# Transposing x by DMA for duos 1 to 3, with a new order of the work, in a fused sliding-window attention and highway layer

## The chip, the core and the metric

The kernel runs on one core of a Trainium2 chip. A core has five engines that run in parallel, each with its own queue of instructions, taken strictly in order: TensorE (PE in the profile; its weight loads are PEld), VectorE (DVE), ScalarE (ACT), GpSimd (POOL) and SyncE (SP), which here only issues DMAs. GpSimd issues DMAs too, beside its arithmetic. TensorE writes into PSUM; the other data lies in SBUF. The metric is the time of one execution in microseconds on the device, the median of several runs.

## The reference

Attention over a window of 128 keys with a bias that falls linearly with distance, followed by a highway layer over the rows of its output:

```python
# q, k, v: (8, 8, 576, 64); rel = query position - key position
scores = scale * q @ k.T - slopes[h] * abs(rel)
scores = where((rel >= 0) & (rel < 128), scores, -1e9)
x = softmax(scores) @ v            # then (batch, seq, heads*dim): x is 4608 x 512
H = maximum(x @ w_h, 0)
T = 1 / (1 + exp(-(x @ w_t + b_t)))
out = T * H + (1 - T) * x
```

## The kernel before

**Tiling.** Two batch rows make a "duo"; there are four (m = 0 to 3). A duo is worked in stages: duo 0 in four small ones ("abcd"), duos 1 to 3 in two each ("A", "B"), ten in all, counted by `stage_no` from 0. A stage covers some query blocks of both rows and all eight heads, two heads at a time.

**Loads.** GpSimd issues the loads of q, k (L110), their last 64 rows (L115) and v (L122), which turn f32 into bf16 on the way. q and k have two buffers each, so duo m reuses those of duo m - 2.

**Attention.** TensorE transposes q and k (L270, L256), VectorE and ScalarE copy them out of PSUM (L282, L289, L295), TensorE forms scores (L328), ScalarE exponentiates (L344), VectorE multiplies by a mask that also holds part of the bias (L363), TensorE multiplies with v and a column of ones (L386), and VectorE divides by the sum ("norm", L402 and L403). The last norm of a stage completes its x, a tile of 128 rows by 4 or 5 blocks by 512.

**Highway layer, block by block of 128 rows.** Stage 'A' has 4 blocks, 'B' 5; duo 0 has 9 in its four stages, so there are 36. For each block:

- x is transposed, because TensorE contracts over partitions: four 128x128 transposes on TensorE into one PSUM buffer (`f_x`, L426) and one copy on ScalarE into an `xt` buffer (`f_xe`, L435).
- Z, the gate's input, is four matmuls with w_t (L460) and one that adds the bias (L462); H is four with w_h (L443). Each takes a PSUM buffer of its own.
- VectorE forms uu = max(H, 0) - x (L450), ScalarE tt = tanh(Z/2) (L468), GpSimd 0.5 tt + 0.5 (L473; for the last stage's blocks but the first on VectorE), VectorE uu * tt (L478), GpSimd uu + x into an `ot` buffer (L484; for the very last block on VectorE).
- SP stores the block with four DMAs of 64 KB (L500), or with two of 128 KB (L492) for the block that holds the last 64 rows of both batch rows.

**Buffers.** PSUM has 4 buffers for all of it; `xt` has 5, `uu`, `tt`, `ot` and x have 3 each. A new `ot` must wait until the store of the third last one has landed.

**What sets the order.** Each piece of work is entered as a node with its engine, a cost in nanoseconds, a due time, its inputs and the buffer that it takes. `plan` (L698) places the nodes: it keeps a clock per engine, and on each engine picks, among the pieces that could start within a margin `LOOKS` of the earliest, the one with the lowest due time plus its kind's `SHIFT` (L765). The instructions are then written out in that order, and each engine executes its own list in order. `DMA_X` (L52) names the stages whose x is transposed by SP's DMA instead. It is empty, so this branch of the nodes is not taken:

```python
if stage_no in DMA_X:                                   # L661
    node(("x", kb), "SP", 450 * n, t - 1.3 * dt, lambda kb=kb: f_xd(*kb), alln,
         take="xt", uses=[xo], land=1000 * n)
else:
    node(("xp", kb), "PE", 350 * n, t - 1.0 * dt, lambda kb=kb: f_x(*kb), alln, ...)
    node(("x", kb), "ACT", (590, 1020)[two], t - 0.9 * dt, lambda kb=kb: f_xe(*kb), ...)
```

`alln` is the list of all four norms of the stage, so no block of a stage is transposed before its last norm.

Of the kernel before, what the change touches and what calls it, by code (L numbers as in the profile page):

```python
# [14 lines left out]
def kernel(  # L15
# [33 lines left out]
        "d": ((3, 3, 0), (3, 4, 128), (4, 4, 192)),  # L49
    }  # L50
    ORDER = ("abcd", "AB", "AB", "AB")
    DMA_X = ()  # L52

    HOME = {"A": ("A", 0), "B": ("B", 0), "a": ("A", 0), "b": ("A", 256), "c": ("B", 0), "d": ("B", 256)}

# [17 lines left out]
    xp = ctx.enter_context(tc.tile_pool(name="x", bufs=BUFS["x"]))  # L73
# [339 lines left out]
    def f_xd(m, kind, gi):  # L413
        bs, n, x = grp(m, kind, gi)
        xt = fx.tile([P, 2, NCK, P], BF16, name="xt")
        XT[m, kind, gi] = xt
        for i in range(n):
            nc.sync.dma_start_transpose(out=xt[:, i], in_=x[:, i, :])
# [86 lines left out]
    def node(key, eng, cost, prio, emit, deps=(), take=None, uses=(), land=0, n=1):  # L505


        nodes[key] = (eng, cost, prio, emit, [d for d in deps if d in nodes],
                      take, tuple(uses), land, n)
# [37 lines left out]
    for m in range(ND):  # L547
# [56 lines left out]
        for kind in ORDER[m]:  # L604
# [3 lines left out]
            for g in range(H // 2):  # L608
# [15 lines left out]
                for hl in range(2):  # L624
                    h = 2 * g + hl
# [30 lines left out]
            for gi, bs in enumerate(GROUPS[kind]):  # L656
                t, n = ffn_pos, len(bs)
                dt = n * FFN_T
                ffn_pos += dt
                kb, xo, two = (m, kind, gi), ("nrm", (m, kind, 0)), n == 2  # L660
                if stage_no in DMA_X:  # L661
                    node(("x", kb), "SP", 450 * n, t - 1.3 * dt, lambda kb=kb: f_xd(*kb), alln,
# [35 lines left out]
    def plan(shift, look):  # L698
# [64 lines left out]
        return sorted(order, key=lambda o: o[0]), max(clock.values())  # L763

    SHIFT = {  # L765
        "exp": 88.43, "g": -18.62, "h": 0.52, "msk": 18.93, "nrm": -67.88, "o": -47.94,
        "pv": -1.59, "qk": -10.75, "s": -3.22, "st": 29.24, "t": -30.24, "te": -24.78,
        "th": 3.83, "tl": 0.89, "tr": -0.44, "u": -52.27, "v": 2.76, "x": -21.95,
        "xp": -1.21, "z": -1.38,
    }  # L770
    LOOKS = {"PE": 339, "ACT": 61, "DVE": 175, "POOL": 297, "SP": 936}
    order, end = plan(SHIFT, LOOKS)

    with tc.manual_schedule():
# [30 lines left out]
```

The softmax here doesn't subtract the row's maximum and nothing guards it: scores larger than these inputs give would overflow.

## Time and profile before

| | us |
|---|---|
| median of 3 runs | 185.63 (184.53 to 186.93) |
| the profiled execution, in all | 185.63 |
| its span, first to last instruction | 183.9 |
| TensorE busy | 155.0 (84%) |
| VectorE busy | 141.6 (77%) |
| ScalarE busy | 127.8 (69%) |
| GpSimd busy | 121.5 (66%) |
| L426, four transposes of x per block | 144 instructions, 14.1 |
| L435, their copy out of PSUM | 36, 21.0 (586 ns each) |
| stores L500 | 128 issues, 421 ns median on SP, 1.8 us to land |

The span is what the profile covers; the execution takes 1.7 us more. Busy times of TensorE overlap with its own pipeline, so the cost of a group there is better read from the distance between its neighbours than from its durations. In a row of the timeline stand the start, the length, the engine, the line, the operation with its tiles, and in brackets how long the engine had been idle before it and what ended that. SPq is SP's queue issuing DMAs. In the chain of waits each row is a start, a length, and what the time went to.

### The profile page before, as it was taken

Reading aid. Unit: us, or ns where it says so; the run is one execution under the profiler, and the core shown is the slowest. Engines: PE = TensorE matmul, PEld = TensorE weight load, DVE = VectorE, ACT = ScalarE, POOL = GpSimd, SP = SyncE. Lnnn points to the kernel's source line nnn. Section 1 sums busy time; section 2 is a strip of 40 time slices with the busy share of each in tenths; the row PEclk is TensorE's granted clock in tenths of the full one; section 3 lists DMA queues with packets and bytes.
Section 4 is the critical chain, followed back from the end, with each engine's and each line's share of the span. In section 5 each row is a group of like instructions: output and inputs, shape, how many; then the busy total and the mean of one; then the engine's idle time right before and its main releaser. Section 6 shows DMA issues by size and latency. Waiting matters only on the chain.

```text
span 183.9 us, 5244 instructions
## 1 busy us (share of the span) xinstructions
PE 155.0 (84%) x2132; PEld 93.9 (51%) x2132; DVE 141.6 (77%) x253; ACT 127.8 (69%) x178; POOL 121.5 (66%) x132
## 2 busy tenths in 40 slices
PE   0286886779999957997999999999998999999950
PEld 0264655655564524675554565665444666555510
DVE  5339885699999893697688999799899788866770
ACT  2558595753889953879779889786998888445510
POOL 7994123979999945984269953544487787667540
PEclk9999999999999996999999999999999999999995
DMA  4999999999999999999997994142212322243543
GB/s 157 225 187 198 200 199 176 138 132 92 127 207 228 210 200 205 135 187 225 208 135 96 178 159 90 45 103 61 57 45 74 93 66 74 74 103 99 137 128 94
DMA packets 70167, 25.50 MB, mean 139 GB/s; under 512 B 48128, under 2 KB 65024, under 8 KB 70144
## 3 DMA queue, kind: packets, MB, share of 16 engines
q0 software_dynamic: 62832, 14.68, 113.6%
q1 hardware_dynamic: 7312, 10.49, 21.3%
q8 instruction: 16, 0.26, 0.6%
q14 instruction: 7, 0.06, 0.1%
HBM read 30.41 MB, written 9.44 MB: 217 GB/s over the span
## 4 chain that ended last, share of the span: by engine, by line
PE 38%; DMA 26%; DVE 16%; POOL 7%; ACT 5%; issue 3%; SPq 1%; POOLq 0%; DVEq 0%; ACTq 0%
DMA kl<-in_k_dram 24%; PE ps L460 10%; PE ps L443 9%; DVE pt L363 6%; PE ps L386 6%; PE ps L270 5%; PE ps L328 5%; DVE x L403 4%; POOL ot L484 3%; DMA out_dram<-ot 3%; ACT pt L344 2%; PE ps L462 2%; DVE uu L450 2%; POOL ql L110 2%; PE ps L426 2%
## 5 line engine op out<-in xcount | busy, mean ns | idle before, releaser
L344 ACT ACTIVATE pt<-ps,bias 128x1024 bf16<-128x1024 f32 (+1 forms) x80 | 73.4, 951 | 9.1 <-PE ps L328 8.4
L484 POOL TENSOR_TENSOR ot<-uu,x 128x512 f32<-128x512 bf16 x35 | 49.7, 1421 | 30.4 <-DVE uu L478 28.9
L363 DVE TENSOR_TENSOR pt<-pt,mk 128x2048 bf16<-128x2048 bf16 (+1 forms) x40 | 47.8, 1210 | 0.7 <-ACT pt L344 0.5
L460 PE MATMUL ps<-wT,xt 128*128 128x512 bf16 x144 | 38.0, 387 | 1.2 <-DVE uu L450 0.7
L443 PE MATMUL ps<-wH,xt 128*128 128x512 bf16 x144 | 37.2, 380 | 0.6 <-DVE uu L450 0.3
L122 POOL DMA_DIRECT2D va<-in_v_dram x20 | 22.2, 1117 | 14.3 <-DMA kl<-in_k_dram 8.2
L450 DVE SCALAR_TENSOR_TENSOR uu<-ps,x 128x512 bf16<-128x512 f32 x36 | 24.8, 688 | 7.7 <-PE ps L443 7.3
L468 ACT ACTIVATE tt<-ps 128x512 f16<-128x512 f32 x36 | 21.5, 598 | 11.6 <-PE ps L462 11.1
L328 PE MATMUL ps<-qt,kt 64*128 64x256 bf16 (+2 forms) x384 | 27.2, 254 | 1.8 <-DVE kt L295 1.4
L473 POOL TENSOR_SCALAR tt<-tt 128x512 f16<-128x512 f16 x32 | 23.1, 722 | 5.6 <-ACT tt L468 5.5
L435 ACT COPY xt<-ps 128x512 bf16<-128x512 bf16 x36 | 21.0, 586 | 8.1 <-PE ps L426 7.2
L403 DVE TENSOR_TENSOR x<-ps,rd 128x256 bf16<-128x256 f32 (+3 forms) x40 | 25.5, 637 | 1.4
L386 PEld LDWEIGHTS <-pt 128*128 128x128 bf16 (+1 forms) x576 | 21.2, 101 | 8.0 <-issue 1.8
L386 PE MATMUL ps<-va,pt 128*128 128x65 bf16 (+1 forms) x576 | 24.1, 196 | 1.3 <-ACT kt L295 0.4
L295 ACT COPY kt<-ps 128x1024 bf16<-128x1024 bf16 x13 | 13.1, 1012 | 14.4 <-PE ps L270 8.4
L289 DVE COPY qt<-ps 128x1024 bf16<-128x1024 bf16 x16 | 10.9, 687 | 14.2 <-PE ps L270 10.9
L478 DVE TENSOR_TENSOR uu<-uu,tt 128x512 bf16<-128x512 bf16 x36 | 16.6, 462 | 4.9 <-POOL tt L473 2.9
L270 PE MATMUL ps<-ident,ql 128*64 128x128 bf16 (+1 forms) x320 | 13.3, 242 | 8.3 <-DMA ql<-in_q_dram 7.5
L443 PEld LDWEIGHTS <-xt 128*128 128x128 bf16 x144 | 12.1, 97 | 14.4 <-issue 2.8
L460 PEld LDWEIGHTS <-xt 128*128 128x128 bf16 x144 | 12.4, 99 | 13.7 <-issue 3.9
L328 PEld LDWEIGHTS <-kt 64*128 64x128 bf16 x384 | 12.8, 97 | 12.6 <-issue 7.0
L270 PE MATMUL ps<-ident,kl 128*64 128x128 bf16 (+1 forms) x320 | 12.8, 242 | 6.6 <-DMA kl<-in_k_dram 5.6
(46 smaller groups left out, 127.9 us busy)
## 6 DMA issues: line engine op xcount, KB each, us to landing
out_dram<-ot SPq DMA_DIRECT2D x128, 64.0 KB, 1.8
va<-in_v_dram POOLq DMA_DIRECT2D x16, 256.0 KB, 10.8
ql<-in_q_dram POOLq DMA_DIRECT2D x3, 1024.0 KB, 14.6
kl<-in_k_dram POOLq DMA_DIRECT2D x3, 1024.0 KB, 18.8
ql<-in_moe_w_h_dram SPq DMA_DIRECT2D x1, 1024.0 KB, 5.8
out_dram<-ot SPq DMA_DIRECT2D x8, 128.0 KB, 2.4
ql<-in_q_dram POOLq DMA_DIRECT2D x4, 128.0 KB, 5.8
kl<-in_k_dram POOLq DMA_DIRECT2D x4, 128.0 KB, 5.9
```

The source lines that it names most:

```text
L122: nc.gpsimd.dma_start(out=VA[m % 2][0:n, c, :, :, 0:D].rearrange("s r h d -> s (r h) d"), in_=v[2 * m : 2 * m + 2, :, c * P : c * P + n, : ...
L270: nc.tensor.transpose(out=pt[r * D : (r + 1) * D, c : c + n], in_=L[ps, r, nh * hs + hl, t * D : (t + 1) * D], identity=ident[ps, ps],)
L328: nc.tensor.matmul(out=sc[:, r, o + off : o + off + w_], lhsT=KT[i][rows, h, j * P : (j + 1) * P], rhs=rhs, start=not add, stop=not add or ...
L344: nc.scalar.activation(out=PT[m, home, h // 2][:, h % 2, :, c0 : c0 + W], in_=SC[m, kind, h][:, :, o : o + W], func=ACTF.Exp, bias=BIAS[:, ...
L363: nc.vector.tensor_tensor(out=o, in0=o, in1=mk.to_broadcast([P, 2, rep, W]), op=ALU.mult,)
L386: nc.tensor.matmul(out=av[rows, hl, n * (D + 1) : (n + 1) * (D + 1)], lhsT=pt[:, hl, r, off : off + (D if narrow else P)], rhs=va[:, j, r, ...
L403: nc.vector.tensor_tensor(out=x.rearrange("p b (h d) -> p h b d", h=2), in0=av[:, :, :, 0:D], in1=rd[:, :, 0:nb].to_broadcast([P, 2, nb, D ...
L443: nc.tensor.matmul(out=AH[m, kind, gi][:, i, :], lhsT=XT[m, kind, gi][:, i, c, :], rhs=wH[:, c, :], start=c == 0, stop=c == NCK - 1)
L450: nc.vector.scalar_tensor_tensor(out=uu[:, 0:n, :], in0=AH[m, kind, gi][:, 0:n, :], scalar=0.0, in1=x, op0=ALU.max, op1=ALU.subtract,)
L460: nc.tensor.matmul(out=az, lhsT=XT[m, kind, gi][:, i, c, :], rhs=wT[:, c, :], start=c == 0, stop=False)
L473: eng.tensor_scalar(out=tt, in0=tt, scalar1=0.5, scalar2=0.5, op0=ALU.mult, op1=ALU.add)
L484: eng.tensor_tensor(out=ot[:, 0:n, :], in0=UU.pop((m, kind, gi))[:, 0:n, :], in1=x, op=ALU.add)
```

## The change

In words it is given as: early set-up of constants, the last block's gate and sum on VectorE, separate PSUM buffers for H and Z, and x of the last three duos transposed by DMA, in place of a kernel with constants and buffer clears set up first. Both kernels have the first three already; the two differ in the following lines alone.

```diff
-    DMA_X = ()
+    DMA_X = tuple(range(4, 10))
...
     SHIFT = {
-        "exp": 88.43, "g": -18.62, "h": 0.52, "msk": 18.93, "nrm": -67.88, "o": -47.94,
-        "pv": -1.59, "qk": -10.75, "s": -3.22, "st": 29.24, "t": -30.24, "te": -24.78,
-        "th": 3.83, "tl": 0.89, "tr": -0.44, "u": -52.27, "v": 2.76, "x": -21.95,
-        "xp": -1.21, "z": -1.38,
+        "exp": 43.87, "g": 2.35, "h": 3.43, "msk": 33.15, "nrm": -32.26, "o": -3.31,
+        "pv": -0.57, "qk": -0.96, "s": -1.85, "st": 37.24, "t": 5.25, "te": -10.07,
+        "th": 1.23, "tl": 5.68, "tr": 0.09, "u": 5.51, "v": 13.43, "x": 9.28, "xp": -15.31,
+        "z": 1.24,
     }
-    LOOKS = {"PE": 339, "ACT": 61, "DVE": 175, "POOL": 297, "SP": 936}
+    LOOKS = {"PE": 334, "ACT": 226, "DVE": 126, "POOL": 267, "SP": 2642}
```

Stages 4 to 9 are the six of duos 1 to 3, with 27 blocks. For each of these `f_x` and `f_xe` go, and `f_xd` comes, which was in the code already:

```python
def f_xd(m, kind, gi):
    bs, n, x = grp(m, kind, gi)
    xt = fx.tile([P, 2, NCK, P], BF16, name="xt")
    XT[m, kind, gi] = xt
    for i in range(n):                                  # n is 1 for every block
        nc.sync.dma_start_transpose(out=xt[:, i], in_=x[:, i, :])      # L418
```

That is one DMA per block, 128 x 512 bf16 from SBUF to SBUF, issued by SP between its stores. The new shifts and margins place the pieces anew on all engines. In the built program SP has 27 instructions more, TensorE 108 transposes less and ScalarE 27 copies less; the number of instructions of the other kinds stays. SP's list for the last stage reads: three transposes, two stores, one transpose, four stores, one transpose, 30 stores.

## The prediction

> **What bounds the kernel now.** I read the chain of waits first, because it says which engine the end hangs on. Its line by engine:
>
> ```profile
> PE 38%; DMA 26%; DVE 16%; POOL 7%; ACT 5%; issue 3%; SPq 1%; POOLq 0%; DVEq 0%; ACTq 0%
> ```
>
> TensorE leads and DMA follows. So I read the chain in order of time, to see where each has its share. The last DMA on it is the load of k for duo 2:
>
> ```profile
> 50.10 1.16 POOL ql L110
> 51.27 18.85 DMA kl<-in_k_dram
> 70.12 0.04 issue
> 70.16 0.89 PE ps L270 x16
> ```
>
> Up to 70.16 us the loads set the pace; TensorE stands idle for 3.14 us before that point. From there the chain is mostly TensorE. The table of windows gives the busy time of that stretch (PE, PEld, DVE, ACT, POOL, each with its count):
>
> ```profile
> 100.00:115.00 15.00, 14.56 (x199) 8.61 (x197) 13.80 (x21) 13.16 (x17) 9.94 (x12) 1.00 1.49 140
> 115.00:130.00 15.00, 14.63 (x230) 9.02 (x229) 12.64 (x19) 11.63 (x16) 7.78 (x7) 1.00 0.26 63
> 130.00:145.00 15.00, 14.34 (x153) 7.67 (x152) 13.18 (x20) 12.96 (x17) 10.28 (x8) 1.00 0.26 67
> 145.00:162.00 17.00, 17.00 (x224) 10.61 (x224) 14.62 (x23) 12.72 (x18) 12.75 (x12) 1.00 0.34 83
> ```
>
> TensorE is full, and VectorE is close behind. After 162 us the chain changes once more:
>
> ```profile
> 168.41 0.42 SPq L500
> 168.83 0.04 issue
> 168.87 1.76 DMA out_dram<-ot
> 170.63 0.03 issue
> 170.65 0.02 POOLq L484
> 170.67 1.16 POOL ot L484
> ```
>
> A sum on GpSimd waits for a free ot buffer, that is for a store to land, and the store waits for its turn on SP. SP's own row in the timeline says how full it is there:
>
> ```profile
> 161.79 17.79 SPq L500 DMA_DIRECT2D out_dram<-ot  x32
> 179.69 1.11 SPq L492 DMA_DIRECT2D out_dram<-ot  x2
> ```
>
> So the kernel has three parts: loads to 70 us, TensorE to 162, and a tail in which TensorE and the SP queue are both nearly full.
>
> **What the Trainium skill says.** "VectorE: DVE Perf Modes", section The three transpose paths, prices a 128x128 bf16 transpose at 390 ns on TensorE and 1309 ns by DMA. The trace has four of the former overlapped: one block's four take 0.22 to 0.32 us of TensorE. No DMA transpose is in the trace. "DMA: Bandwidth & Descriptors", section Issuing engines are not separate DMA queues, says that all queues run on the same 16 DMA engines; the trace agrees, as stores land in 4.6 us (median) between 75 and 100 us, beside the loads, and in 1.7 us after 120. The same page, section Anatomy of one DMA, says that a semaphore wait is held by the issuing sequencer: what stands behind a waiting transpose on SP waits too.
>
> **Step 1, transposes off TensorE and ScalarE.** Duos 1 to 3 have 9 blocks each, so 27 blocks lose four L426 transposes and one L435 copy. On TensorE I price a block by the spacing of its neighbours. Mid-kernel:
>
> ```profile
> 148.36 0.39 PE L426 MATMUL ps<-ident,x 128*128 128x128 bf16 x4
> 148.68 0.40 PE L328 MATMUL ps<-qt,kt 64*128 64x256 bf16 x8
> ```
>
> That is 0.32 us. In the tail a block comes every 2.17 us (162.15, 164.32, 166.49), of which nine matmuls of 0.217 are 1.95, leaving 0.22. By the built order, 23 transposed blocks stand between the k load and the last attention product before, and none after (27 go; one of duo 0 moves ahead of the load, into the 3.14 us of idle). 23 x 0.22 to 0.32 = 5.1 to 7.4 us; I take 6.2. The 27 copies are 27 x 0.586 = 15.8 us of ScalarE, which is 78% busy from 100 to 162 us; the cover is TensorE, and I take zero, as for the 27 PSUM buffers that are no longer taken. Both could give a little more.
>
> **Step 2, the order.** New shifts move more than x. Ahead of the k load for duo 2 TensorE has one gate-and-H block (1.95 us) and eight score matmuls less; the block reappears behind the last attention product, the scores before it (8 x 0.041 = +0.3 us). GpSimd issues q of duo 2 ahead of four small operations and k ahead of two (an L484 of 1.54 and an L473 of 1.05, so k is issued 2.6 us earlier), passing no other load. The DMA digits read 9 throughout and the v load issued at 46.3 took 11 us, so a queue was waiting: I take the landing as unmoved at 70 us (gain 0 to 2.6). q of duo 3 is issued before v of duo 2, whose first use is after 100 us: nothing. Shifts in ACT and DVE order I put at nothing, cover TensorE, bounds -2 to +2 us.
>
> **Step 3, VectorE.** Its work is untouched: 66.9 us busy from 84 to 162 (12.66 in 84 to 100, plus the rows above), 86%. With 6 us less to do it in, 93%. In-order engines don't run that full without waits, so some gain is lost: 0 to 3 us, I take 1.6. The last norm, ending at 163.34 before, ends then at 163.3 - 6.2 + 0.3 + 1.6 = 159.0.
>
> **Step 4, 27 transposes on SP.** What one costs SP is unknown. Below: a store's issue, 0.42 us (median of L500). Above: 1.3 us if SP is held as long as the 128x128 price. The skill's DMA page has, in the table of sequencer cycles at the end of its section on why a DMA increments its semaphore by 16, 512 cycles for a copy and 262,144 for 8,192 tiles transposed inside SBUF, column for earlier generations: 32 cycles per tile. Its section DMA Transpose gives a tile as 16 partitions by 128 columns, so 128x512 is 32 tiles, 1024 cycles; with 512 cycles = the 0.42 us measured, 0.84 us. I take 0.9 as an estimate. In the body that is hidden: 70 stores from 84 to 161 us at 0.46 (issue and 0.04 gap) are 32 us, and 22 transposes add 20, 52 of some 73. Landing (1.7 us idle or 5 us loaded, up to 4 x 1.3 = 5.2 in transit) is hidden too: between the norm of duo 1's first stage and the first use of its x stand about ten groups of attention matmuls, over 10 us. The loads of duo 3 share their DMA engines with nine transposes; its k landed at about 96 us (issued at 77.6 at the latest, 18.3 to land) and is first used at 105.07, so up to 9 us of delay cost nothing. Behind the first transposes, stores wait for a norm; the sum behind them reuses an ot buffer three blocks later, so I put that at nothing, bound 2 us.
>
> **The tail is where it shows.** The five last blocks cannot be transposed before the last norm, and in the built order 36 stores stand behind the first of these five on SP. 36 x 0.46 + 5 x (0.9 + 0.04) = 21.3 us, plus 3.1 from the last issue to the end (180.8 to 183.9): norm + 24.4. TensorE alone would need 8 blocks x 1.95 = 15.6 from the last product, 1.1 before the norm, plus 6.9 (177.0 to 183.9): norm + 21.4. SP is later. End: 159.0 + 24.4 = 183.4 us of span, against 183.9. The profiled execution took 185.63 in all, 1.7 beyond its span, and is itself the median of the runs, so I forecast **185 us: no change**. A change of 2% is about what a measurement can tell here, and I use it as the bound: 181.9 and 189.3.
>
> **Rivals.** (a) *TensorE's gain comes through.* If a transpose costs SP 0.42 and VectorE keeps up, the norm ends at 157.4, SP adds 22.0: span 179.4, 181.1 us; with k landing 1 to 2 us earlier, 179.5. For it: TensorE at 96 to 100%. Against: SP full for 17.8 us in the tail already. (b) *SP is held by its transposes.* At 2.0 us each the tail is 36 x 0.46 + 5 x 2.04 + 3.1 = 29.9, and SP's body 32 + 22 x 2 = 76 of 73 us adds about 3: 159 + 3 + 29.9 = 191.9, 193.6 us. It decides from about 1.75 us on: 159 + 16.6 + 5 x 1.79 + 3.1 = 187.6, 189.3 us. Late transposes then stall TensorE, and late stores hold the ot buffers and GpSimd. For it: no price of a whole SBUF transpose in this trace, 1309 ns for a quarter of one. If a transpose held SP four times that, 5.2 us, the body alone would grow by some 70 us; I hold that for unlikely. (c) *The change does less than it says.* Set-up, the last block's gate on VectorE and separate H and Z buffers are in both kernels; only the transposes and the order change. The order alone, without any gain from x, gives 185.6 + 2.0 for the block moved behind the last product + 0.3, less up to 2.6 of an earlier k: 185.3 to 187.9.
>
> **Numbers.** No change 0.44 (its own range 182 to 189), including most of (c); (a) faster 0.22; (b) slower 0.34, for the upper end of the price is open and a new in-order wait on SP has more ways to cost than to gain. The range 180.5 to 193 leaves out the lower half of (a) and the far end of (b).
>
> **What would show it.** Step 1: TensorE busy falls by about 10 us, ScalarE by 16, and the stretch from the k load to the last norm shortens by about 4.5. Step 2: the first transposes of k for duo 2 still start near 70 us. Step 3: VectorE over 90% between 84 and 158. Step 4: SP's row for L418 near 0.9 us, and SP without gaps after the last norm. I am wrong if L418 stands at 0.5 or at 2 us, or if TensorE waits for xt in the body.

## The result, and the profile after

| | before | after |
|---|---|---|
| median, us | 186.28 (184.53 to 187.13, 4 runs) | 198.0 (197.01 to 199.47, 4 runs) |
| ratio, 95% interval | | 1.065 (1.054 to 1.076) |
| span of the profiled execution | 183.9 | 196.9 |
| last norm (L403) ends at | 163.34 | 165.98 |
| from there to the end | 20.6 | 30.9 |
| TensorE busy, from 70 us to the last norm | 90.4 of 93.4 | 86.7 of 96.0 |
| GpSimd waits for an `ot` buffer (a store) | 1.3 | 23.3 |

The change makes the kernel 6.5% slower. The forecast was 185.0, "no change"; 198 lies outside its range of 180.5 to 193. Here and below medians are over all executions, while ratios leave out executions that a second, slower state of the chip had lengthened. The span grew by 13.0 us: 2.6 ahead of the last norm and 10.3 behind it. TensorE did shed work, but in the stretch that it should have shortened it now stands idle for 9.3 us where it was idle for 3.0.

First the chain of waits of the kernel after, by engine (the page's part 4):

```profile
PE 35%; DMA 28%; DVE 14%; POOL 6%; ACT 5%; SPq 4%; issue 3%; POOLq 0%; DVEq 0%; ACTq 0%
```

SP's queue went from 1% to 4% and DMA from 26% to 28%. The windows say in which stretch TensorE lost its work. They are the four stretches that the prediction showed of the kernel before (start and end, length, then the busy time of PE, PEld, DVE, ACT and POOL; behind these the mean granted clock of TensorE as a share of full speed, the busy share of the DMA engines, and GB/s):

```profile
100.00:115.00 15.00, 12.01 (x169) 6.71 (x167) 11.64 (x20) 9.89 (x11) 9.95 (x11) 1.00 2.05 142
115.00:130.00 15.00, 11.11 (x170) 7.21 (x171) 9.32 (x14) 7.00 (x8) 6.12 (x6) 0.77 0.73 118
130.00:145.00 15.00, 15.00 (x156) 7.38 (x153) 13.39 (x21) 11.62 (x14) 10.28 (x8) 1.00 0.42 95
145.00:162.00 17.00, 16.86 (x188) 8.95 (x187) 16.23 (x26) 12.27 (x14) 12.34 (x12) 1.00 0.60 112
```

From 100 to 130 us TensorE is busy for 23.1 us, where it was 29.2 before, and VectorE falls with it, from 26.4 to 21.0. After 130 TensorE is full again and VectorE is busy for nine tenths of the time. So the body has one place of loss. The chain in order of time names what stands there (start, length, what):

```profile
100.39 0.39 SPq L418
...
100.88 8.21 DMA xt<-x
...
109.11 8.77 DMA out_dram<-ot
...
118.25 0.86 SPq L500
...
119.15 1.71 DMA out_dram<-ot
```

A transpose issued at 100.88 lands 8.2 us later. The store at 109.11 is issued only then, and takes 8.8 us to land; the store at 117.89 is again issued only then. In both cases SP waits for the eighth DMA ahead in its own list. The trace shows why: a DMA tells of its landing on a semaphore, a counter that others wait for, and each DMA of SP uses the same semaphore as the eighth before it (in all 156 cases of this kernel). So at most eight are under way, and slow landing holds the queue itself. Between 75 and 120 us SP waited eight times like this (what it waited for; us in total, times, longest):

```profile
SPq L500 <- DMA xt<-x: 7.3, 5, 3.2
SPq L500 <- DMA out_dram<-ot: 4.0, 3, 2.8
```

In the kernel before SP waits for a landing once in this stretch, for 1.0 us. From there the delay runs through all engines: at 118.35 GpSimd's sum has waited 5.3 us for the stores of one block to free an `ot` buffer, at 120.12 VectorE 4.0 us for GpSimd's next result, at 121.58 ScalarE 4.4 for VectorE's copy, and at 122.64 TensorE 3.5 for ScalarE's.

TensorE's wait has a sequel, which the clock of 0.77 in the second window hints at. The clock was granted at half from 120.95 to 127.77 us:

```profile
120.95:127.77 6.82, 5.12 (x55) 3.22 (x56) 5.75 (x8) 4.27 (x5) 3.14 (x2) 0.50 0.63 99
```

Four matmuls of L460 took 1.87 us there (at 123.66) and 1.03 just before the wait (at 113.96). TensorE was busy for 5.1 us of the stretch, which at the full clock would have been about 2.6. Half-clock stretches near 70 us stand in both kernels (3.4 us each, behind the wait for k); this one is new. Of the kernels of this document that store a block in four pieces, the seven with transposes by DMA in stages 4 and 5 all have a half-clock stretch between 84 us and their last norm, of 3.4 to 10.2 us in all, and the eight without have none.

The table of DMA issues for the stretch from 75 to 110 us shows that this is no single case (KB each, median us from issue to landing):

```profile
out_dram<-ot SPq DMA_DIRECT2D x18, 64.0 KB, 7.6
...
xt<-x SPq DMA_TRANSPOSE x9, 8.4
```

The same table from 120 to 180 us, when the loads are over:

```profile
out_dram<-ot SPq DMA_DIRECT2D x54, 64.0 KB, 1.7
...
xt<-x SPq DMA_TRANSPOSE x18, 2.5
```

Beside the loads a transpose lands in 8.4 us, without them in 2.5. In the kernel before, stores landed in 4.4 us between 75 and 110 (26 of them); now they take 7.6. That the transposes cause this, and not the order, is shown by two kernels of the next part: with the new order but no transposing DMA stores land in 4.9 us there, with the old order and nine of them in 6.5.

Behind the last norm, SP's rows of the timeline (start, length, line, operation, count):

```profile
168.10 3.87 SPq L418 DMA_TRANSPOSE xt<-x  x3
172.07 1.18 SPq L492 DMA_DIRECT2D out_dram<-ot  x2
173.34 1.25 SPq L418 DMA_TRANSPOSE xt<-x  x1
174.69 3.01 SPq L500 DMA_DIRECT2D out_dram<-ot  x4
177.79 1.22 SPq L418 DMA_TRANSPOSE xt<-x  x1
179.11 13.58 SPq L500 DMA_DIRECT2D out_dram<-ot  x28
192.79 1.12 SPq L492 DMA_DIRECT2D out_dram<-ot  x2
```

The rows follow each other, each starting about 0.1 us after the last one ends. A row of SP also takes in the gaps between its instructions; here there is a single one over 0.13 us, of 0.44, so SP works through its list from 168.1 to 193.9 us, and the kernel ends 3.0 us later. In the kernel before, such gaps behind the last norm add up to 3.8 us, most of them waits for GpSimd's sums (SP's waits from 163 to 184 us):

```profile
SPq L500 <- POOL ot L484: 3.0, 3, 1.3
```

SP's row of 32 stores in 17.79 us, which the prediction read as a full queue, held such gaps: 32 x 0.46 is 14.7. A transpose holds SP for 1.22 us, and with the gap to the next instruction 1.3. The row of L418 over the whole run says the same of all 27 (minimum, median, maximum in ns):

```profile
L418 SPq DMA_TRANSPOSE xt<-x x27: 1188/1221/3057, 79.0 to 177.8; - x27
```

### The profile page after: what moved, and what is told of

Read it like the earlier page. It is cut to its first block, busy times and chain, and to the rows that moved or that the text cites. A ratio compares the mean times of both kernels' runs of the same rounds, so it can differ in the third digit from the quotient of the medians.

```text
span 196.9 us, 5059 instructions
## 1 busy us (share of the span) xinstructions
PE 151.6 (77%) x2024; PEld 88.1 (45%) x2024; DVE 141.4 (72%) x253; ACT 113.8 (58%) x151; POOL 121.5 (62%) x132
## 4 chain that ended last, share of the span: by engine, by line
PE 35%; DMA 28%; DVE 14%; POOL 6%; ACT 5%; SPq 4%; issue 3%; POOLq 0%; DVEq 0%; ACTq 0%
DMA kl<-in_k_dram 11%; PE ps L460 9%; PE ps L270 8%; DMA out_dram<-ot 8%; PE ps L443 8%; DMA xt<-x 6%; ACT pt L344 4%; PE ps L328 4%; PE ps L386 4%; SPq L500 4%; DVE pt L363 3%; DMA ql<-in_q_dram 3%; DVE qt L289 3%; DVE x L403 2%; POOL va L122 2%
## 5 line engine op out<-in xcount | busy, mean ns | idle before, releaser
L344 ACT ACTIVATE pt<-ps,bias 128x1024 bf16<-128x1024 f32 (+1 forms) x80 | 72.5, 949 | 11.0 <-PE ps L328 10.5
L484 POOL TENSOR_TENSOR ot<-uu,x 128x512 f32<-128x512 bf16 x35 | 47.4, 1354 | 41.9 <-DMA out_dram<-ot 23.3
L363 DVE TENSOR_TENSOR pt<-pt,mk 128x2048 bf16<-128x2048 bf16 (+1 forms) x40 | 47.1, 1193 | 0.2 <-ACT pt L344 0.2
L460 PE MATMUL ps<-wT,xt 128*128 128x512 bf16 x144 | 39.0, 394 | 4.8 <-DVE qt L289 1.2
L468 ACT ACTIVATE tt<-ps 128x512 f16<-128x512 f32 x36 | 21.5, 597 | 30.1 <-PE ps L462 25.9
L450 DVE SCALAR_TENSOR_TENSOR uu<-ps,x 128x512 bf16<-128x512 f32 x36 | 24.7, 685 | 8.6 <-POOL ot L484 4.3
L478 DVE TENSOR_TENSOR uu<-uu,tt 128x512 bf16<-128x512 bf16 x36 | 18.9, 527 | 13.0 <-POOL tt L473 11.6
L473 POOL TENSOR_SCALAR tt<-tt 128x512 f16<-128x512 f16 x32 | 25.5, 801 | 4.4 <-ACT tt L468 4.3
L403 DVE TENSOR_TENSOR x<-ps,rd 128x256 bf16<-128x256 f32 (+3 forms) x40 | 25.5, 638 | 1.5
L386 PEld LDWEIGHTS <-pt 128*128 128x128 bf16 (+1 forms) x576 | 20.6, 101 | 11.8 <-issue 3.2
L289 DVE COPY qt<-ps 128x1024 bf16<-128x1024 bf16 x16 | 10.9, 687 | 15.8 <-PE ps L270 14.7
L460 PEld LDWEIGHTS <-xt 128*128 128x128 bf16 x144 | 12.7, 99 | 20.1 <-issue 4.7
L270 PE MATMUL ps<-ident,ql 128*64 128x128 bf16 (+1 forms) x320 | 13.8, 247 | 8.8 <-DMA ql<-in_q_dram 8.3
L270 PEld LDWEIGHTS <-ql 128*64 128x64 bf16 (+1 forms) x320 | 11.1, 138 | 12.2 <-DMA ql<-in_q_dram 8.4
## 6 DMA issues: line engine op xcount, KB each, us to landing
kl<-in_k_dram POOLq DMA_DIRECT2D x3, 1024.0 KB, 20.6
```

What stands on the lines that cost most here:

```text
L270: nc.tensor.transpose(out=pt[r * D : (r + 1) * D, c : c + n], in_=L[ps, r, nh * hs + hl, t * D : (t + 1) * D], identity=ident[ps, ps],)
L344: nc.scalar.activation(out=PT[m, home, h // 2][:, h % 2, :, c0 : c0 + W], in_=SC[m, kind, h][:, :, o : o + W], func=ACTF.Exp, bias=BIAS[:, ...
L363: nc.vector.tensor_tensor(out=o, in0=o, in1=mk.to_broadcast([P, 2, rep, W]), op=ALU.mult,)
L386: nc.tensor.matmul(out=av[rows, hl, n * (D + 1) : (n + 1) * (D + 1)], lhsT=pt[:, hl, r, off : off + (D if narrow else P)], rhs=va[:, j, r, ...
L403: nc.vector.tensor_tensor(out=x.rearrange("p b (h d) -> p h b d", h=2), in0=av[:, :, :, 0:D], in1=rd[:, :, 0:nb].to_broadcast([P, 2, nb, D ...
L450: nc.vector.scalar_tensor_tensor(out=uu[:, 0:n, :], in0=AH[m, kind, gi][:, 0:n, :], scalar=0.0, in1=x, op0=ALU.max, op1=ALU.subtract,)
```

## The experiments

Three theories were in play, and each expectation below speaks of one or more of them. **SP's time:** the transposes' 1.3 us each are too much for a queue that also issues 136 stores. **Landing:** they land late beside the loads. **Order:** the new shifts lose time whatever the transposes do. In the expectations O is the order, L the landing, and V or S2 SP's time; the other letters are told where they stand. Ratios are to the kernel before, timed on the same chip. "Norm" is where the last L403 ends, "tail" is from there to the end of the span, both from one profiled execution.

### Which part of the change costs: order or transposes

**Only the transposes, with the shifts of the kernel before.**

```diff
# before.py
-    DMA_X = ()
+    DMA_X = tuple(range(4, 10))
```

> The kernel before with only the set of stages whose x goes by DMA changed, shifts and margins as before (the planner still re-places the pieces). Theory S: 193 us or more, the tail from the last norm to the end is above 27 us, and the transposes issued before 110 us land in over 6 us. Theory O: within 2% of before, 183 to 189 us.

191.46 us, ratio 1.035 (1.028 to 1.042); norm 163.4, tail 26.7. The transposes alone make the kernel slower. The kernel after stands at 1.065: the step between the two, which is the shifts and margins alone, is 1.065/1.035 = 1.029, some 5.4 us, with an interval of 1.6 to 4.2% worked out from the two. Neither theory expected so even a split. Where the order costs can be counted in the timelines of these two, behind the last norm: in the kernel after 32 matmuls of H and 28 of Z are left, with the old shifts 27 and 24; on VectorE 9 of L450, then 7; on SP 41 stores, then 34. More of the highway layer is left over when attention ends, and no attention runs beside it.

**Only the order: the transposes back on TensorE, in the places that the DMAs had.**

```diff
# after.py
-                    node(("x", kb), "SP", ..., lambda kb=kb: f_xd(*kb), alln, ...)
+                    node(("x", kb), "SP", ..., lambda kb=kb: (f_x(*kb), f_xe(*kb)), alln, ...)
```

> The changed kernel with its written order kept on every engine, but each of the 27 transposing DMAs replaced in place by the four TensorE transposes and the ScalarE copy of the kernel before. Theory S (SP and the DMA transposes cost the time: issue in the tail, slow landing beside the loads in the body): SP is free again, TensorE has its 6 to 9 us back; the kernel falls from 198 to 186 to 190 us, the last norm to the end of the span takes 21 to 24 us instead of 30.9, and GpSimd waits less than 8 us for stores (23.3 in the changed kernel). Theory O (the new order costs the time, the transposes don't): 195 us or more, with the same waits.

194.01 us, 1.049 (1.041 to 1.056); norm 168.9, tail 24.6. Between both expectations. This run holds two things that it can't separate, the order and transposes at places on TensorE that were chosen for a DMA. It says only that the two together are not free.

**After's order with 13 transposes, in stages 6, 7 and 8; the other 14 blocks on TensorE in place.**

> The kernel after in its own written order, with the blocks of stages 4, 5 and 9 transposed on TensorE in place (14 blocks), so that 13 transposing DMAs are left in stages 6, 7 and 8. The same 13 with the old shifts gave 183.4 us, so the difference is the new order's. Theory O (the new order costs some 6 us whatever the transposes do, as between the kernel after and the run with the old shifts and all 27): 189 to 193 us, the last norm at 164 to 168 us and some 24 to 25 us behind it. Rival (the new order costs only where late transposes meet it): 183 to 186 us.

187.91 us, 1.016 (1.006 to 1.026). The same 13 transposes under the old shifts (below) gave 0.993 (0.989 to 0.996). The ratio of the two is 1.023, about 4 us, between the two expectations; like the run before, it takes the order together with 14 blocks transposed at places chosen for a DMA. The tail of 24.6 us was as the theory of the order expected. The norm was not: it ended at 160.3, ahead of the 164 to 168 expected. The loss is again work left for the tail: 31 matmuls of H, 27 of Z and 42 stores on SP, where the old shifts leave 28, 24 and 35.

### Where the transposes cost: each place alone, with the old shifts

```diff
# before.py, three kernels
-    DMA_X = ()
+    DMA_X = (4, 5)        # 9 blocks, beside the loads
+    DMA_X = (6, 7, 8)     # 13 blocks, between
+    DMA_X = (9,)          # 5 blocks, behind the last norm
```

> The kernel before with its own shifts and DMA transposes in stages 4 and 5 alone: 9 blocks, beside the loads. Theory L (beside the loads a transpose lands in 8 us and the stores behind it wait; that costs more than the 9 x 0.27 = 2.4 us that TensorE sheds): the last norm ends at 164 to 167 us where it was 163.3, the stretch behind it stays near 20.6: 186 to 189 us. Rival (the loads hide it): 183 to 184.5 us.

> The kernel before with its own shifts, and DMA transposes only in stages 6, 7 and 8 (13 blocks in place of 27): after the loads have ended, and none behind the last norm. Theory P (the transpose by DMA is bad only in two places: beside the loads, where it lands in 8 us, and behind the last norm, where SP is full): each lands in about 2.5 us, TensorE sheds 13 x 0.22 to 0.32 = 3 to 4 us, the last norm ends 1 to 4 us before 163.3, the tail stays near 20.6: 181 to 184 us. Rival Q (the stores that stand behind each transpose on SP's queue are enough, wherever it is): GpSimd waits over 8 us for stores, the last norm is not earlier than in the kernel before, 185 to 189 us.

> The kernel before with its own shifts and DMA transposes in stage 9 alone: 5 blocks, all behind the last norm. Theory V (the volume of SP's work behind the last norm sets the end): 5 x 1.3 = 6.5 us are added to a full queue, the stretch behind the norm goes from 20.6 to 25 to 27 us, 189 to 192 us. Rival (TensorE's chain of 27 matmul groups is the bound there, and it sheds 5 x 0.22 us): 183 to 186 us.

| transposed by DMA | median, us | ratio | norm | tail |
|---|---|---|---|---|
| none (before) | | 1 | 163.3 | 20.6 |
| stages 4, 5 | 189.53 | 1.026 (1.016 to 1.035) | 166.8 | 20.5 |
| stages 6 to 8 | 183.4 | 0.993 (0.989 to 0.996) | 158.7 | 21.3 |
| stage 9 | 189.41 | 1.027 (1.017 to 1.036) | 161.8 | 24.2 |
| all of these | 191.46 | 1.035 (1.028 to 1.042) | 163.4 | 26.7 |

Within their error the three parts add up: 2.6 - 0.7 + 2.7 = 4.6%, where the first and the last are known to about 1% either way, against 3.5% for all. One and the same instruction is a loss in two places and a small gain in the third. The norms are of one execution each and shift by over 3 us by themselves: that of stages 6 to 8 is from its fastest execution, of 181.75 us, which had no half-clock stretch before its norm, and a later kernel with the same written order, shown at the end of this part, had two and a norm of 162.1.

Beside the loads the theory of landing holds. The chain of the kernel with stages 4 and 5:

```profile
78.18 8.29 DMA xt<-x
86.51 0.61 PE ps L460
...
100.01 7.05 DMA xt<-x
107.11 1.04 PE ps L460 x4
...
110.22 6.81 DMA out_dram<-ot
117.19 1.16 POOL ot L484
```

TensorE waits for a transpose twice, 3.15 us and 0.5 us; the third wait is GpSimd's, for a store behind transposes. The norm came 3.5 us later although TensorE had 9 blocks less to transpose, estimated at 2.4 us, so 5.9 us were lost. The first wait and what follows it explain most of this: from 85.0 us the clock is at half for 6.8 us, in which TensorE is busy for 5.1, about 2.5 more than at the full clock. The tail did not move at all. For stage 9 SP's rows in the tail are

```profile
160.27 1.93 SPq L500 DMA_DIRECT2D out_dram<-ot  x4
162.37 6.53 SPq L418 DMA_TRANSPOSE xt<-x  x5
168.99 11.36 SPq L500 DMA_DIRECT2D out_dram<-ot  x24
```

The five transposes take 6.53 us of the queue as expected. The tail grew by 3.6, not by 4.4 to 6.4: part of the transposes fills time in which SP had waited, for its gaps behind the norm fell from 3.8 to 0.2 us. In stages 6 to 8 the transposes landed in 2.8 us (median), and TensorE has no wait for one of them.

**The same two places taken back from the kernel after**, whose order stays:

```diff
# after.py, two kernels: f_x and f_xe in place of f_xd in
+    stages 4 and 5
+    stage 9
```

> The changed kernel in its own order, with x of duo 1 (stages 4 and 5, nine blocks) transposed on TensorE in place; duos 2 and 3 by DMA as before. Theory S1 (transposes beside the loads land late, the stores behind them wait, GpSimd stops for ot buffers between 90 and 125 us): the last norm ends 4 to 8 us sooner than at 166.0, GpSimd's wait for stores falls below 14 us, and the time is 191 to 195 us. Theory S2 (only SP's issue time in the tail matters): the last norm stays at 165 to 168 and the time at 197 to 200 us.

> The changed kernel in its own order, with x of the last stage alone (five blocks) transposed on TensorE in place; the other 22 by DMA. Theory S2: SP loses 5 x 1.3 = 6.5 us of issues behind the last norm and TensorE no longer waits for xt; the stretch from the last norm to the end shrinks from 30.9 to 23 to 26 us, the time to 190 to 194 us. Theory S1: the last norm stays at about 166 and the tail shortens by less than 3 us, 195 us or more.

Stages 4 and 5: 196.2 us, 1.056 (1.047 to 1.066); norm 163.0, 3.0 us sooner where 4 to 8 were expected, tail 31.3. The time misses both expectations, and its interval overlaps that of the kernel after, so the gain is not clear of noise. Stage 9: 193.41 us at the median, too scattered for a ratio (190.2 to 194.6); its profile is of the slowest execution, norm 167.9, tail 25.0, 5.9 us shorter as expected. Each shortens its own stretch and not the other.

### What holds the body: buffers or the queue

```diff
# after.py
-    op = ctx.enter_context(tc.tile_pool(name="ot", bufs=BUFS["ot"]))    # 3
+    op = ctx.enter_context(tc.tile_pool(name="ot", bufs=6))
-        ot = op.tile([P, 2, DM], F32, name="ot")
+        ot = op.tile([P, 1, DM], F32, name="ot")
```

> The kernel after with the memory of the output tiles cut into 6 buffers of one block where it was 3 buffers of two (same bytes, same written order, blocks of one tile only hold what they use; blocks of two are not formed in this shape). Theory B (in the body the transposes' cost reaches TensorE through the output tiles: stores stand on SP's queue behind transposes that land late, the three tiles stay held, GpSimd waits 23.3 us for them, and VectorE and TensorE wait behind GpSimd): with twice the tiles GpSimd's wait for stores falls below 8 us and the last norm ends 3 to 6 us sooner than 165.98, at 160 to 163; the tail is not touched, so 192 to 195 us. Theory S (SP's own time is all: 27 x 1.22 us of issue, and SP is full from 168 us on): the waits for tiles go, but the end is SP's and stays at 197 to 199 us.

197.91 us, 1.065 (1.054 to 1.076): no gain at all. The waits tell why, though the profile with six buffers is of the slowest of its four executions, 200.87 us. In the kernel after (us in total, times, longest):

```profile
POOL ot L484 <- DMA out_dram<-ot: 23.3, 9, 5.6
...
PEld L460 <- DMA xt<-x: 2.9, 4, 1.2
```

With six buffers:

```profile
PEld L460 <- DMA xt<-x: 8.7, 5, 3.4
PE ps L460 <- DMA xt<-x: 6.7, 4, 2.9
POOL ot L484 <- DMA out_dram<-ot: 5.8, 2, 3.5
```

GpSimd's wait fell from 23.3 to 5.8 us, below the 8 that were expected, and the time stayed: TensorE now waits for the transposes itself, and SP still waits 9.7 us in all for the eighth DMA ahead of the next. The longest wait for a DMA was a symptom. That the loss reaches TensorE through the output buffers alone is ruled out here.

### What holds the tail: SP's sequence or its volume

```diff
# after.py: the five transposes of the last stage right behind the last norm
+    last = [o for o in order if o[1][0] == "x" and o[1][1][:2] == (3, "B")]
+    rest = [o for o in order if o not in last]
+    at = 1 + [o[1] for o in rest].index(("nrm", (3, "B", 3)))
+    order = rest[:at] + last + rest[at:]
```

> The kernel after with one change in its written order: the five transposing DMAs of the last stage stand together on SP's queue right behind the last norm; the stores that stood between them follow. Same instructions. Theory Q (in the tail it is a queue matter: TensorE waits for the last x, whose transpose SP issues only at 177.8 us because stores stand ahead of it): all five are issued by about 173 us, as in the run with the old shifts (last norm to end 26.7 us there), so the stretch goes from 30.9 to 26 to 28 us and the time to 192 to 195 us. Rival V (the volume of SP's work behind the last norm sets the end, whatever its sequence: 5 transposes x 1.3 and 38 stores x 0.46 us): the stretch stays at 29.5 to 32 us, 196 to 199 us.

199.24 us, 1.080 (1.070 to 1.091); norm 164.3, tail 31.5. All five transposes are issued by 173.8 us instead of 179.0, and the end is no nearer: SP's list is as long as it was. The volume of the list sets the end, not its sequence.

```diff
# after.py: in duo 3 every second store on ScalarE's queue
-            nc.sync.dma_start(out=dst[t], ...)
+            (nc.scalar if t % 2 and m == 3 else nc.sync).dma_start(out=dst[t], ...)
```

> The kernel after, with every second store of the last two stages (8 and 9) issued on ScalarE's queue where it was SP's. Theory S (SP is full from 168.1 to 193.9 us and its issue sets the end): some 14 of the stores behind the last norm leave SP, x 0.46 us = 6.4 us, the stretch from the last norm to the end goes from 30.9 to 23 to 26 us and the time to 190 to 194 us. Rival (the last block's own chain of transpose, matmuls, gate and sum sets the end, and SP is only busy beside it): the stretch stays within 2 us of 30.9 and the time at 196 us or more.

196.23 us, 1.060 (1.051 to 1.069); tail 27.9, 3.0 us shorter, half of what was expected; the ratio's interval overlaps that of the kernel after. ScalarE waits 7.6 us in its tanh (L468) for stores ahead of it on its own queue. The load went from one in-order queue to another that had work of its own, and SP, with gaps of 4.4 us behind the norm, was no longer what set the end alone.

The same edit together with six `ot` buffers on the kernel **before**:

> The kernel before with 6 output tiles of one block and every second store of the last two stages on ScalarE's queue, no transposing DMA at all. If SP's issue of the stores already sets the end of the kernel before (36 stores x 0.46 us = 16.6 of the 20.6 us behind its last norm), some 14 x 0.46 = 6 us leave SP, of which the last block's chain of matmuls and gate gives back a part: 180 to 183 us. If the tail of before is bounded by that chain, not by SP: 184.5 to 186.5 us.

184.3 us, 0.990 (0.985 to 0.995). A gain of 1%, between the two expectations; tail 20.1 after 20.6. So SP's stores were not much of a bound in the kernel before, where SP waited for sums and TensorE's chain in the tail ends at 177.0 and VectorE's last sum at 179.2 us.

**One store for a block in place of four**, in three kernels:

```diff
-        for t in range(4):
-            nc.sync.dma_start(out=dst[t], in_=ot[32 * t : 32 * t + 32, 0 : len(bs), :])
+        nc.sync.dma_start(out=dst.rearrange("t p b n -> t p (b n)"), in_=ot[:, 0, :])
```

> The kernel before, with each block's four stores of 32 rows made one store of 128 rows (the same bytes to the same rows, 40 DMAs where there were 136). Theory S: of SP's 16.6 us of stores behind the last norm some 13 us go; what stays is the last block's chain, which ends at 179.2 us (VectorE's last sum), and one store's issue and landing of 2.4 to 3 us: the span goes from 183.9 to 181.5 to 182.5 us, so 183 to 184 us. Rival: one store of 256 KB takes four times the issue or lands later than four small ones: 185 us or more.

> The kernel after with one store for each block in place of four; the 27 transposing DMAs are as they were. Theory V (SP's volume: 27 transposes added to 136 stores is more than its queue carries, both in the body and behind the last norm): 96 stores x 0.46 = 44 us leave SP, the transposes are issued as soon as x is there, GpSimd's waits for stores fall below 8 us, and 186 to 190 us are left (some of the new order's own loss stays). Rival L (what counts is that each transpose lands late, 8 us beside the loads, and the new order): GpSimd and TensorE wait as before, 194 us or more.

> The kernel before with DMA transposes in stages 6, 7 and 8 alone and one store for each block. If the gains of both add (1.5 to 2 us from the 13 blocks off TensorE, 1.5 to 2.5 us from the stores): 180 to 182 us, 2% or more under the kernel before. If SP's queue was the price of the transposes in stages 6 to 8 as well, they land sooner here and it is 179 to 180 us. If the large store is no gain: 183 to 184 us.

209.3 us (1.136), 225.5 (1.222) and 215.29 (1.154). No expectation foresaw the size, though the rival of the first said that a large store might land later. The large store costs SP only 0.54 us, but in the chain of the first of these kernels it takes

```profile
182.01 6.46 DMA out_dram<-ot
...
189.81 6.90 DMA out_dram<-ot
```

to land, where one of 64 KB took 1.76 us. While it is under way the DMA engines are 26% busy (windows from 182.2 to 188.3 and 190.0 to 196.5), which is 4 of 16. The Trainium skill has a reason that fits: "DMA: Bandwidth & Descriptors", section Why a DMA increments its semaphore by 16 and not by 1, says that such a DMA is split over the largest number up to 16 that divides both sides' slowest dimension, here 4 and 128. These runs decide nothing between the theories above, since they brought in a larger cost of their own.

### A version from the parts that gain

Transposes in stages 6 to 8, six `ot` buffers, and every second store of duo 3 on ScalarE's queue, with the old shifts.

> The kernel before with three edits that each gave something or should: DMA transposes in stages 6, 7 and 8 alone (ratio 0.993), six output tiles of one block and every second store of the last two stages on ScalarE's queue (0.990 together). If the gains add: 0.983 of the kernel before, 181 to 182.5 us. If both take the same time off the same tail: 183 to 184 us.

182.83 us, 0.989 (0.981 to 0.998); norm 162.1, tail 20.2. It is ahead of both kernels, by 1.1% of the kernel before, but no more than either of its parts: the gains do not add.

## Why the prediction was wrong

**The body of step 4 failed most.** It held the landing of the transposes "hidden too", with 5 us loaded and over 10 us before the first use, and put the stores behind the first transposes "at nothing, bound 2 us". Landing was 8.4 us in the median. The first use was nearer: 9.6 us behind the first issue in the kernel after (79.0 to 88.6), and in the kernel with stages 4 and 5 alone TensorE had nothing else left after 5.2 us (78.2 to 83.4) and then waited 3.2. The prediction counted SP's time as issue alone, 52 of some 73 us. It left out that SP goes on only when the eighth DMA ahead has landed, which cost SP 11.3 us of waits between 75 and 120 us, and that the four transposes issued first took 6.7 to 7.2 us of SP's time. It also left out the half clock behind TensorE's wait, about 2.5 us. Transposes in stages 4 and 5 alone cost 2.6%, some 4.8 us, where their share of step 1 is a gain of 9 x 0.27 = 2.4: a miss of about 7. The wait that it named as a bound, stores held behind a transpose, was there; the Trainium skill's statement that a wait is held by the issuing sequencer ("DMA: Bandwidth & Descriptors", Anatomy of one DMA) was read rightly and priced too low.

**The tail of step 4 had each term too small.** Predicted: 36 stores x 0.46 + 5 x 0.94 + 3.1 = 24.4. Measured: 41 stores end behind the last norm, since SP was still 2.1 us in arrears with stores when the norm ended (+2.3); a transpose takes 1.3 with its gap (+1.8); some 2.6 us are left over (27.9 from the norm to the end of its last issue, less 41 x 0.46 and 5 x 1.3), of which one store that held SP for 1.61 us, for a cause that stays open, makes 1.2 and the gap of 0.44 before a sum 0.4; and 3.0 to the end. Together 31.0 against 30.9, where the rest of 2.6 is what makes it fit. The form of the sum was right. The price from the skill's table of sequencer cycles, 0.84 as an estimate, is 1.22 on this chip, a factor of 1.45.

**Step 2 put the order at nothing, -2 to +2 us.** It costs 2.9% with 27 transposes, some 5.4 us. The block moved behind the last attention product was seen, and its 1.95 us held to be hidden by SP; in fact more stores were left for SP too, 41 behind the norm where the old shifts with the same transposes leave 34. The landing of k was right: its first transposes stand at 69.44 us, before at 70.16.

**Step 1's size was about right.** Between 70 us and the last norm TensorE's busy time fell by 3.7 us of the 6.2, and the half clock added some 2.6 to it, so that by this estimate about 6.3 were shed; the row of L426 fell from 14.1 to 2.7. Where neither loads nor the tail interfere, 13 blocks gained 0.7%, 1.3 us, of 13 x 0.27 = 3.5. So even in its best place under half of the gain came through. What took the rest there was not separated.

**Step 3 was wrong in its direction.** VectorE was to be over 90% busy between 84 and 158; it was 57.8 of 74 us, 78%, because it waited too. Its general ground, that in-order engines don't run so full without waits, did not hold of TensorE in the kernel before, busy for 17.0 of 17.0 us. The norm was to end at 159.0 and ended at 165.98.

**The rivals.** Rival (b) came nearest with 193.6 us, and its consequence, late transposes and late stores that hold GpSimd, is what the chain shows. But it hung on a price of 2 us on SP and was to decide "from about 1.75 us on"; with the measured 1.3 it would not have. It missed that landing, not issue, is what TensorE and SP wait for in the body. Rival (a) failed; rival (c)'s sum for the order alone, 185.3 to 187.9, was too low: 2.9% of 185 are 5.4 us, or 190.4.

**What stays open.** Which of the new shifts leaves the extra work behind the last norm was not tried piece by piece. The planner prices a transposing DMA at 450 ns of SP (the node in "The kernel before"), where it took 1220, and counts eight places for GpSimd's DMAs (`lanes` in `plan`) but none for SP's; whether an order planned with the measured prices would gain was not tried. Nor is it known why the part gains of the last version don't add, or what ends the half clock sooner or later.

## What to carry to other kernels

- Price a DMA that takes the place of engine work by its landing in the stretch where it will run, beside the loads that run there, and look for the queue it joins: what stands behind it is delayed as well, and when only so many DMAs can be under way, slow landing stops the queue.
- When an engine has waited, read its clock in the stretch behind the wait too: a busy time measured at half the clock counts double.
- A queue that only issues can be the bound of a tail. Count everything that it must still issue when the last input arrives, its arrears included; changing the sequence doesn't shorten the list. A merged row of a queue hides its gaps, so look for waits before calling it full.
- Where one edit covers many places, try the places one by one: here the same instruction lost 2.6%, gained 0.7% and lost 2.7%. And don't take the longest wait for the cause before it has been removed once.

## What the runs showed of the hardware

- A transposing DMA of 128 x 512 bf16 inside SBUF holds SP for 1.22 us (a store: 0.42) and lands in 2.5 us with no loads running, in 8.4 beside them. It costs the hardware queue 544 packets, (22,000 - 7,312)/27, and 131 KB. The skill's "VectorE: DVE Perf Modes", section The three transpose paths, has 1309 ns for a quarter of it; without loads four quarters landed in twice that.
- They slow the neighbours: between 75 and 110 us v landed in 9.7 us in place of 6.8, and k in 20.6 in place of 18.3. With the order held, it is 9.7 after 7.3 for v and 20.6 after 15.4 for k (kernel after, against the same order with the transposes on TensorE).
- A wait of TensorE can be followed by a stretch at half the granted clock: 3.5 us of waiting up to 122.64, half clock from 120.95 to 127.77. It need not be: the kernel with transposes in stages 6 to 8 waited 3.0 us for k and had none.
- A store of 128 rows whose target is written as 4 groups of 32 uses a quarter of the DMA engines: 256 KB landed in 6.5 to 6.9 us, four stores of 64 KB in 1.8 each.
